# Softcap attention, ReLU² MLP and top-1 experts on one core: a division moved up, sixteen copies moved to ScalarE, the extra tile's weights in another order, and two small float32 products in float32r

## The chip, the core and the metric

The kernel runs on one core of a Trainium2 chip. TensorE multiplies (PE; its weight loads are a row of their own, PEld), VectorE (DVE) and ScalarE (ACT) do elementwise work, GpSimd (POOL) does a little of it and the indirect DMAs, and SyncE (SP) issues most of the other DMAs. The metric is the device time of the whole program in microseconds (us); lower is better. The time before is 510.29 us, the median of 3 runs (509.88 to 512.22). One more execution was taken with the profiler: it took 511.6 us, of which 509.9 us lie between its first and last instruction (the span, in which the trace counts its times).

## The reference

Three stages follow each other; the output of one is the input of the next. There are 2 x 448 = 896 tokens, 12 heads of 64, a model width of 768.

```python
# q, k, v: [2, 12, 448, 64]
scores = cap * tanh((q @ k.T) / 8 / cap)          # softcap attention, per head
attn = exp(scores - max); attn /= attn.sum(-1) + 1e-9
x = (attn @ v) as [896, 768]

h = maximum(x @ w_in, 0)                           # MLP: w_in [768, 2048], w_out [2048, 768]
x = (h * h) @ w_out

xn = x / (norm(x) + 1e-6); en = emb / (norm(emb) + 1e-6)   # 8 experts, top 1
logits = xn @ en.T / tau                           # [896, 8]
e = argmax(logits); gate = softmax(logits)[e]
out[row] = gate * (maximum(x[row] @ w1[e], 0) @ w2[e])     # w1 [8, 768, 1024], w2 [8, 1024, 768]
```

## The kernel before

**Number format.** A float32 matrix is held as two float32r tiles: a rounded high part (`xh`, `wh`, `gh`, ...) and the remainder (`xl`, `wl`, `gl`, ...). A product is three TensorE passes, high by high, high by low and low by high (`pass3`, lines 584 to 587). Small products whose operands are not split go to TensorE as plain float32.

**Stages.** The work is cut by batch b (0 and 1, 448 tokens each), and each stage of one batch is interleaved with the next stage of the other:

1. attention of batch 0 (12 heads, in 6 pairs, lines 376 to 574);
2. `mlp(0)` with attention of batch 1 between its matmuls;
3. `mlp(1)` with the router of batch 0;
4. `expert(0)` with the router of batch 1, and the preparation of the extra tile;
5. `expert(1)` with the extra tile.

`mlp(b)` has 16 h blocks (one per 128 columns of w_in: 6 x 3 matmuls of 448 columns, then ReLU and square) and 6 y blocks. `square` (line 598) squares on ACT, rounds the square into `gh` on DVE (line 603), and subtracts for `gl` on DVE (line 604). A block's square is issued when the next block has done three of its six steps.

**Attention.** A step g scores two blocks of keys (`scores`), prepares later heads (`fronts(g + 2)`: casts `qh`, `kh` and the transposed `tq`, mostly on DVE), and multiplies weights with v (`values(g)`, L471, plain float32). When a pair of heads m is complete, `divide(m)` (lines 483 to 493) reads the two PSUM banks of the pair on DVE: row sums `rs`, reciprocal, and two products into `rows`. Two steps later `finish(m)` (line 495) transposes `rows` on TensorE (`xp`, L508) into `xt`, the input of the MLP; its own remainder `xl` is written by DVE one step after (the `late` list). The banks that `divide` reads are the banks that the next pair's `values` write.

**Weights.** A chunk is a piece of a weight matrix. It passes the stages load (DMA on SP), conv (w_in and w_out lie in memory as 64-bit numbers and are turned into float32 by ACT L231 and DVE L214, L215, L217), store (of the float32 copy, for batch 1), and split (`wh` by ACT L237 or DVE L239, `wl` by DVE L243). `pump(n)` moves the stages of coming chunks on when chunk n is taken, and puts their instructions in a list; `drip` issues one of the list at each step of the main loop. Before `mlp(0)` the attention loop calls `pump` with n from -6 up to 0 (lines 1105 to 1108). From `expert(0)` on, even chunks lie in a pool of 2 buffers for each of `wf`, `wh` and `wl`, odd chunks in a pool of 4.

**Experts.** For each batch the expert that most of its tokens chose is computed densely for all 448 tokens: 20 chunks, 8 of w1 (`e` blocks, 18 matmuls each) and 12 of w2 (`z`, 6 column blocks of two chunks). So blocks 0 to 19 are batch 0, 20 to 39 batch 1. Tokens of other experts are gathered, 64 at a time, in an extra tile of its own weights: 12 chunks of w1 (128x512, products `xo`) and 8 of w2 (128x768, products `xy`). `XAT` (line 182) says after which block each of the 20 is used. `extra_next` (line 1167) lets the extra tile take one step at each block's end.

**The extra tile's rows** (`ys`, 64 rows) go to the output by an indirect DMA, except the last 256 columns of rows of batch 1: these are placed into the dense rows on TensorE by a 0/1 matrix `smt` (`extra_place`, line 961; `place`, line 1029, product `xm`, L1033, plain float32), and `merged_rows` adds the two.

**Router.** `router(b)` (line 744) multiplies x with the experts' vectors (`lg`, 12 float32r matmuls), and sums the squares of each token with a column of ones (L758, one plain float32 matmul of 448 columns into row 32 of the same bank). Two ACT copies and a POOL memset make `lgs`, which is transposed (`lt`).

What sets the order is the order of the Python code: instructions run in that order on each engine, and wait for each other by semaphores.

Of the kernel before, what the change touches and what calls it, by code (L numbers as in the profile page):

```python
# [20 lines left out]
def kernel(  # L21
# [34 lines left out]
    P = 128  # L56
# [125 lines left out]
    XAT = [18 + i for i in range(12)] + [31, 32, 32, 33, 33, 34, 34, 35]  # L182
# [193 lines left out]
    def attention():  # L376
# [175 lines left out]
        for g in range(G):  # L552
            if g + 2 < G:
                scores(g + 2)
                yield
                yield from fronts(g + 2)
                if g == 1:
                    guard()
            if g:
                yield from values(g)  # L560
            yield
            run_all(late)
            if todo:
                run_all(todo)
                yield
            if 2 <= g < G // 2:
                next(conv, None)
            if g == G // 2:
                run_all(late)
                yield "batch"  # L570
# [21 lines left out]
    def mlp(b):  # L592
# [5 lines left out]
        def square(f, r):  # L598
            if eng["sq"] == "act":
                nc.scalar.activation(r, r, AF.Square)  # L600
            else:
                nc.vector.tensor_tensor(r, r, r, op=ALU.mult)
            nc.vector.tensor_copy(gh[:, f], r)
            nc.vector.tensor_tensor(gl[:, f], r, f32(gh[:, f]), op=ALU.subtract)

        for f in range(NF):
            wh, wl = next_w()
            o = acc(f"h{b}_{f}")
            for cc in range(NCC):
                pass3(o[:, :S], wh[:, cc], wl[:, cc], xh[:, cc], xl[:, cc], cc == 0, cc == NCC - 1)  # L610
                if cc == 2 and late:
                    square(*late.pop())
                yield
            r = ev.tile([P, S], F32, tag="r", name=f"r{b}_{f}")
            nc.scalar.activation(r, o[:, :S], AF.Relu)  # L615
            late.append((f, r))
        square(*late.pop())
        x2h = xp.tile([P, NCC, S], F32R, tag="xh", name=f"x2h{b}")
# [61 lines left out]

    def router_setup():
# [12 lines left out]
        col = small([P, 1], "col")  # L694
        nc.gpsimd.memset(col, 1.0)
# [24 lines left out]
        e2 = small([P, NCC, 2, E], "e2", F32R)  # L720
        nc.vector.tensor_copy(e2[:, :, 0], tp)
        nc.vector.tensor_tensor(e2[:, :, 1], tp, f32(e2[:, :, 0]), op=ALU.subtract)
# [21 lines left out]
    def router(b):  # L744
# [5 lines left out]
        lg = bank("mm", f"lg{b}")  # L750
        for cc in range(NCC):
            w = e2[:, cc].rearrange("p t e -> p (t e)")
            nc.tensor.matmul(lg[:2 * E, :S], w, x2h[:, cc], start=cc == 0, stop=False)
            nc.tensor.matmul(lg[:2 * E, :S], w, x2l[:, cc], start=False, stop=cc == NCC - 1)
        yield

        NR = SQ + 1
        nc.tensor.matmul(lg[SQ:NR, :S], ent["col"], ssq[b], start=True, stop=True)  # L758
        lgs = ev.tile([NR, S], F32, tag="sq", name=f"lgs{b}", bufs=1)
        nc.gpsimd.memset(lgs[:SQ], 0.0)  # L760
        nc.scalar.copy(lgs[:2 * E], lg[:2 * E, :S])
        nc.scalar.copy(lgs[SQ:NR], lg[SQ:NR, :S])
# [5 lines left out]
        nc.vector.tensor_copy(ss, lt[:CP, :, SQ])  # L768
# [192 lines left out]
    def extra_place():  # L961
# [8 lines left out]
        yield  # L970
        tp = ps.tile([P, NC, CP], F32, tag="tr", name="smt_p", bufs=2)
        for c in range(NC):
            nc.tensor.transpose(tp[:T, c], sm[:, (B - 1) * NC + c], ident[:CP, :CP])
        yield
        smt = small([T, NC, CP], "smt")
        nc.vector.tensor_copy(smt, tp[:T])
# [19 lines left out]
    def expert(b, po):  # L996
# [32 lines left out]
        def place(d):  # L1029

            xm = ps.tile([P, NC, P], F32, tag="tr", name=f"xm{d}", bufs=2)
            for c in range(NC):
                nc.tensor.matmul(xm[:CP, c], rt["smt"][:, c], rt["done"][1][:, d * P:(d + 1) * P], start=True, stop=True)  # L1033
# [71 lines left out]
    for i, y in enumerate(att):  # L1105
        drip(2)
        if i >= PS and i % 6 == 0:
            pump(min((i - PS) // 6 - PB, 0))
# [125 lines left out]
```

## Time and profile before

| | |
|---|---|
| median of 3 runs | 510.29 us (509.88 to 512.22) |
| profiled execution | 511.6 us |
| its span | 509.9 us |
| PE busy | 498.4 us, 98% |
| PEld, DVE, ACT, POOL busy | 453.5, 384.8, 261.5, 72.1 us |
| DMA moved | 83.62 MB, mean 164 GB/s |
| chain that ended last | PE 86%, DVE 8%, DMA 3% |

How to read it: PE is busy from the first few microseconds to the last few. A busy PE can still be slowed, since a matmul's bar in the trace ends where the next has already started; what a matmul costs is read from one start to the next start. A stretch in which the starts lie farther apart than elsewhere is a loss that the busy share doesn't show.

### The profile page before, as it was taken

The page shows a single profiled execution, that of the slowest core. Times are in us where ns is not written, and L with a number is a line of the kernel's source. Part 1 is how long each engine was busy: PE and PEld are TensorE (multiplying, and loading weights), DVE is VectorE, ACT ScalarE, POOL GpSimd, SP SyncE. Part 2 cuts the span into 40 slices and gives each one's busy share as a digit, 9 for nine tenths or more (in the row PEclk, how much of TensorE's full clock was granted, in tenths as well). Part 3 has the DMA queues.
Part 4 walks back from the last instruction along what each step waited for, and adds up shares of the span by engine and source line. Part 5 has one row for each costly group of instructions (what it writes and reads, how often), then busy time and mean ns, then how long its engine had stood idle before and what let it go on. Part 6 is the DMA issues. An engine that isn't in the chain of part 4 may idle for free.

```text
span 509.9 us, 8176 instructions
## 1 busy us (share of the span) xinstructions
PE 498.4 (98%) x2814; PEld 453.5 (89%) x2814; DVE 384.8 (75%) x739; ACT 261.5 (51%) x420; POOL 72.1 (14%) x113
## 2 busy tenths in 40 slices
PE   8999999999999999999999999999999999999995
PEld 6899989899999999999998899999789899998984
DVE  6899999799998989896588477666557655456681
ACT  5989986887886674753143340011163213445341
POOL 3645432011110121002001000112100000000000
PEclk9999999999999999999999999999999999999998
DMA  8987959599576887885444123476523477645752
GB/s 127 195 192 161 226 131 244 175 271 279 179 187 200 239 233 207 241 247 160 140 119 125 44 83 95 87 171 179 138 61 74 111 165 166 192 147 158 202 153 55
DMA packets 166956, 83.62 MB, mean 164 GB/s; under 512 B 104050, under 2 KB 154098, under 8 KB 166912
## 3 DMA queue, kind: packets, MB, share of 16 engines
q1 hardware_dynamic: 165056, 82.68, 63.0%
q10 hardware_dynamic: 1728, 0.35, 0.3%
q8 instruction: 23, 0.38, 0.3%
q14 instruction: 21, 0.17, 0.2%
q0 software_dynamic: 128, 0.04, 0.0%
HBM read 65.12 MB, written 18.29 MB: 164 GB/s over the span
## 4 chain that ended last, share of the span: by engine, by line
PE 86%; DVE 8%; DMA 3%; issue 1%; ACT 1%; POOL 0%; DVEq 0%; SPq 0%; ACTq 0%; POOLq 0%
PE pv L471 8%; PE h L585 8%; PE y L585 8%; PE h L586 8%; PE h L587 8%; PE y L587 8%; PE y L586 8%; PE sc L447 5%; PE e L585 4%; PE e L587 4%; PE e L586 4%; PE z L585 3%; PE z L586 3%; PE z L587 3%; DMA wf<-in_moe_w_dram 2%
## 5 line engine op out<-in xcount | busy, mean ns | idle before, releaser
L243 DVE TENSOR_TENSOR wl<-wf,wh 128x512 fp32r<-128x512 f32 (+1 forms) x140 | 113.9, 827 | 43.3 <-ACT wh L237 40.0
L237 ACT CAST wh<-wf 128x512 fp32r<-128x512 f32 (+1 forms) x97 | 65.6, 697 | 39.9 <-PE z L587 25.4
L585 PE MATMUL h<-xh,wh 128*128 128x448 f32 x192 | 71.8, 374 | 0.0
L585 PE MATMUL y<-gh,wh 128*128 128x448 f32 x192 | 71.7, 374 | 0.0
L586 PE MATMUL h<-xh,wl 128*128 128x448 f32 x192 | 70.3, 366 | 0.0
L587 PE MATMUL h<-xl,wh 128*128 128x448 f32 x192 | 70.3, 366 | 0.0
L587 PE MATMUL y<-gl,wh 128*128 128x448 f32 x192 | 70.2, 366 | 0.0
L586 PE MATMUL y<-gh,wl 128*128 128x448 f32 x192 | 70.2, 366 | 0.0
L471 PEld LDWEIGHTS pv<-vt,p_t 128*112 128x112 f32 x576 | 63.1, 178 | 3.4 <-issue 1.4
L471 PE MATMUL pv<-vt,p_t 128*112 128x65 f32 x576 | 62.3, 259 | 1.0 <-issue 1.0
L449 ACT ACTIVATE p_t<-sc,rcap 128x448 f32<-128x448 f32 x84 | 49.2, 630 | 15.0 <-PE sc L447 15.0
L405 POOL TENSOR_TENSOR ql<-tq,qh 64x448 fp32r<-64x448 f32 x22 | 27.5, 1248 | 123.0 <-ACT qh L425 90.4
L453 ACT ACTIVATE p_t<-p_t,capb 128x896 f32<-128x896 f32 x41 | 42.8, 1045 | 1.3
L585 PEld LDWEIGHTS h<-xh,wh 128*128 128x128 f32 x192 | 36.1, 188 | 3.8 <-issue 0.8
L587 PEld LDWEIGHTS h<-xl,wh 128*128 128x128 f32 x192 | 36.1, 188 | 3.2
L587 PEld LDWEIGHTS y<-gl,wh 128*128 128x128 f32 x192 | 36.0, 188 | 3.1
L615 ACT ACTIVATE r<-h 128x448 f32<-128x448 f32 x32 | 17.3, 541 | 41.7 <-PE h L587 26.0
L586 PEld LDWEIGHTS h<-xh,wl 128*128 128x128 f32 x192 | 36.1, 188 | 2.9
L231 ACT ACTIVATE wf<-wr 128x512 f32<-128x512 f32 (+1 forms) x36 | 27.0, 750 | 22.6 <-DMA wr<-in_moe_w_out_dram 7.7
L586 PEld LDWEIGHTS y<-gh,wl 128*128 128x128 f32 x192 | 36.1, 188 | 2.7
L585 PEld LDWEIGHTS y<-gh,wh 128*128 128x128 f32 x192 | 36.1, 188 | 2.7
L447 PE MATMUL sc<-qh,kp 128*128 128x448 f32 x96 | 37.2, 388 | 1.0 <-DVE kp L419 0.4
(247 smaller groups left out, 911.0 us busy)
## 6 DMA issues: line engine op xcount, KB each, us to landing
wr<-in_moe_w_in_dram SPq DMA_DIRECT2D x16, 768.0 KB, 6.0
wr<-in_moe_w_out_dram SPq DMA_DIRECT2D x24, 512.0 KB, 4.7
wf<-in_moe_w_dram SPq DMA_DIRECT2D x24, 384.0 KB, 3.3
wf<-in_moe_w_dram SPq DMA_DIRECT2D x36, 256.0 KB, 3.4
wk<-wf SPq DMA_DIRECT2D x16, 384.0 KB, 6.1
wk<-wf SPq DMA_DIRECT2D x24, 256.0 KB, 4.5
wf<-wk SPq DMA_DIRECT2D x16, 384.0 KB, 4.1
wf<-wk SPq DMA_DIRECT2D x24, 256.0 KB, 3.2
```

The lines of the kernel that those rows point to most:

```text
L231: nc.scalar.mul(c["f"], c["parts"][:, :, :, 1].bitcast(F32), 2.0 ** -112)
L237: nc.scalar.copy(c["hi"], c["f"])
L243: nc.vector.tensor_tensor(c["lo"], c["f"], f32(c["hi"]), op=ALU.subtract)
L405: (nc.gpsimd if n > 1 else nc.vector).tensor_tensor(ql[D:], tq[:D], f32(qh[:D]), op=ALU.subtract)
L447: nc.tensor.matmul(sc[:, :S], h[0][:, c * P:(c + 1) * P], h[x], start=t == parts[0][0] and x == 1, stop=t == parts[-1][0] and x == 2)
L449: nc.scalar.activation(p_t[:, j], sc[:, :S], AF.Tanh, scale=rcap)
L453: nc.scalar.activation(p_t, p_t, AF.Exp, scale=capb)
L471: nc.tensor.matmul(o, w, x, start=i == 0 and t % 2 == 0, stop=i == NK - 1, skip_group_check=True)
L585: nc.tensor.matmul(o, wh, xh, start=first, stop=False)
L586: nc.tensor.matmul(o, wl, xh, start=False, stop=False)
L587: nc.tensor.matmul(o, wh, xl, start=False, stop=last)
L615: nc.scalar.activation(r, o[:, :S], AF.Relu)
```

## The change

Six edits; the tile shapes of the three stages and the number of their large matmuls stay.

1. In attention, at the last step of batch 0 (g + 1 = G/2) `fronts(g + 2)` is issued after `values(g)`, so after `divide`; in batch 1 `finish` is issued directly behind `values` and a step more lies between it and its `xl`.
2. The attention loop calls `pump` five times with n from -6 to -2; the two steps of n = -1 and 0 fall to the first `next_w` of `mlp(0)`.
3. In `mlp(0)` `gh` is written by ACT, and `gl` (new function `low`) is issued two steps later; `mlp(1)` is as before.
4. The router's sum of squares is split in a high and a low float32r part (`sh` by ACT, `sl` by DVE) and summed by two float32r matmuls into row 16 of the same product; one step more lies ahead of them. One ACT copy takes the place of two and of the memset.
5. `XAT` is another: the w1 chunks after blocks 18, 19, two each after 20 to 23, one each after 24 and 25; the w2 chunks one each after blocks 27 to 34 (before: w1 after 18 to 29, w2 after 31, 32, 32, 33, 33, 34, 34, 35).
6. The placement: `ys` (its last 256 columns) as high and low part in 128 rows `y2`, `smt` with 128 rows (each of the 64 twice), so that one float32r matmul takes the place of one float32 matmul. The transposes for it are issued one step earlier, and the copy of `smt` is by ACT.

```diff
-    XAT = [18 + i for i in range(12)] + [31, 32, 32, 33, 33, 34, 34, 35]
+    XAT = [18, 19, 20, 20, 21, 21, 22, 22, 23, 23, 24, 25] + [27 + i for i in range(8)]
...
                 scores(g + 2)
                 yield
-                yield from fronts(g + 2)
+                if g + 1 != G // 2:
+                    yield from fronts(g + 2)
...
             if g:
                 yield from values(g)
+            if g + 1 == G // 2:
+
+                yield from fronts(g + 2)
+            if g > G // 2 and todo:
+                run_all(todo)
+                yield
...
-            nc.vector.tensor_copy(gh[:, f], r)
+            if b:
+                nc.vector.tensor_copy(gh[:, f], r)
+                low(f, r)
+            else:
+                nc.scalar.copy(gh[:, f], r)
+                later.append((f, r))
+
+        def low(f, r):
             nc.vector.tensor_tensor(gl[:, f], r, f32(gh[:, f]), op=ALU.subtract)
...
                 if cc == 2 and late:
                     square(*late.pop())
+                if cc == 4 and later:
+                    low(*later.pop())
                 yield
...
+    NR = 2 * E + 1
...
-        col = small([P, 1], "col")
-        nc.gpsimd.memset(col, 1.0)
+        col = small([P, NR], "col", F32R)
+        nc.gpsimd.memset(f32(col), 0.0)
+        nc.gpsimd.memset(f32(col[:, NR - 1:]), 1.0)
...
         for cc in range(NCC):
-            w = e2[:, cc].rearrange("p t e -> p (t e)")
-            nc.tensor.matmul(lg[:2 * E, :S], w, x2h[:, cc], start=cc == 0, stop=False)
-            nc.tensor.matmul(lg[:2 * E, :S], w, x2l[:, cc], start=False, stop=cc == NCC - 1)
-        yield
-
-        NR = SQ + 1
-        nc.tensor.matmul(lg[SQ:NR, :S], ent["col"], ssq[b], start=True, stop=True)
-        lgs = ev.tile([NR, S], F32, tag="sq", name=f"lgs{b}", bufs=1)
-        nc.gpsimd.memset(lgs[:SQ], 0.0)
-        nc.scalar.copy(lgs[:2 * E], lg[:2 * E, :S])
-        nc.scalar.copy(lgs[SQ:NR], lg[SQ:NR, :S])
+            nc.tensor.matmul(lg, e2[:, cc], x2h[:, cc], start=cc == 0, stop=False)
+            nc.tensor.matmul(lg, e2[:, cc], x2l[:, cc], start=False, stop=False)
+        yield
+        sh = ev.tile([P, S], F32R, tag="sq", name=f"sh{b}", bufs=1)
+        sl = ev.tile([P, S], F32R, tag="xr", name=f"sl{b}")
+        nc.scalar.copy(sh, ssq[b])
+        nc.vector.tensor_tensor(sl, ssq[b], f32(sh), op=ALU.subtract)
+        yield
+        nc.tensor.matmul(lg, ent["col"], sh, start=False, stop=False)
+        nc.tensor.matmul(lg, ent["col"], sl, start=False, stop=True)
+        lgs = ev.tile([NR, S], F32, tag="xr", name=f"lgs{b}")
+        nc.scalar.copy(lgs, lg)
...
         rt["km"] = km
-        yield
+        y2 = small([2 * T, 2 * P], "y2", F32R)
+        yl = ys[:, DM - 2 * P:]
+        nc.scalar.copy(y2[:T], yl)
+        nc.vector.tensor_tensor(y2[T:], yl, f32(y2[:T]), op=ALU.subtract)
+        rt["y2"] = y2
+
+        s2 = small([CP, NC, 2, T], "s2")
+        nc.gpsimd.tensor_copy(s2, sm[:, g].unsqueeze(2).to_broadcast([CP, NC, 2, T]))
         tp = ps.tile([P, NC, CP], F32, tag="tr", name="smt_p", bufs=2)
         for c in range(NC):
-            nc.tensor.transpose(tp[:T, c], sm[:, (B - 1) * NC + c], ident[:CP, :CP])
-        yield
-        smt = small([T, NC, CP], "smt")
-        nc.vector.tensor_copy(smt, tp[:T])
+            nc.tensor.transpose(tp[:, c], s2[:, c].rearrange("p t k -> p (t k)"), ident[:CP, :CP])
+        yield
+        smt = small([2 * T, NC, CP], "smt", F32R)
+        nc.scalar.copy(smt, tp)
...
-                nc.tensor.matmul(xm[:CP, c], rt["smt"][:, c], rt["done"][1][:, d * P:(d + 1) * P], start=True, stop=True)
+                nc.tensor.matmul(xm[:CP, c], rt["smt"][:, c], rt["y2"][:, (d - NCC + 2) * P:(d - NCC + 3) * P],
+                                 start=True, stop=True)
...
-        if i >= PS and i % 6 == 0:
-            pump(min((i - PS) // 6 - PB, 0))
+        if i >= PS and i % 6 == 0 and i < PS + 6 * (PB - 1):
+            pump((i - PS) // 6 - PB)
```

What stands on the engines, at three places. The first is DVE at the end of batch 0's attention: `rs5` and `rows5` are `divide` of the last pair of batch 0, `qh14`, `tq15` and `kp15` prepare heads of batch 1. Before:

```order
L239 CAST wh1_894<-wf1001_447 128x768
L243 TENSOR_TENSOR wl1_896<-wf1001_447,wh1_894 128x768
L423 CAST qh14_839<-tq14_835 64x448
L386 STREAM_TRANSPOSE tq15_901<-qk14_728 128x448
L488 TENSOR_SCALAR rs5_917<-pv5_0_804,ecap_139 112x4
L488 TENSOR_SCALAR rs5_917<-pv5_1_805,ecap_139 112x4
L489 RECIPROCAL rs5_917<-rs5_917 112x8
L492 TENSOR_TENSOR rows5_916<-pv5_0_804,rs5_917 112x256
L492 TENSOR_TENSOR rows5_916<-pv5_1_805,rs5_917 112x256
L423 CAST kp15_903<-tq15_901 64x448
```

And now, on DVE at the same place:

```order
L239 CAST wh1_894<-wf1001_447 128x768
L243 TENSOR_TENSOR wl1_896<-wf1001_447,wh1_894 128x768
L488 TENSOR_SCALAR rs5_907<-pv5_0_804,ecap_139 112x4
L488 TENSOR_SCALAR rs5_907<-pv5_1_805,ecap_139 112x4
L489 RECIPROCAL rs5_907<-rs5_907 112x8
L492 TENSOR_TENSOR rows5_906<-pv5_0_804,rs5_907 112x256
L492 TENSOR_TENSOR rows5_906<-pv5_1_805,rs5_907 112x256
L423 CAST qh14_839<-tq14_835 64x448
L386 STREAM_TRANSPOSE tq15_916<-qk14_728 128x448
L423 CAST kp15_918<-tq15_916 64x448
```

The five instructions of the division stand ahead of the cast `qh14` and the transpose `tq15` instead of behind them. The second place is DVE some 25 us later, in `mlp(0)`: `rs6` and `rows6` are the division of batch 1's first pair, `wf7`, `wf8` and `wl5` weights, `gh0` and `gl0` the parts of a square. Before:

```order
L243 TENSOR_TENSOR wl5_1124<-wf5_965,wh5_1088 128x768
L217 SCALAR_TENSOR_TENSOR wf7_1077<-wr7_971,wf7_1077 128x768
L603 CAST gh0_962<-r0_2_1126 128x448
L604 TENSOR_TENSOR gl0_963<-r0_2_1126,gh0_962 128x448
L214 TENSOR_SCALAR wf8_1129<-wf8_1129 128x768
L488 TENSOR_SCALAR rs6_1170<-pv6_0_935,ecap_139 112x4
L488 TENSOR_SCALAR rs6_1170<-pv6_1_936,ecap_139 112x4
L489 RECIPROCAL rs6_1170<-rs6_1170 112x8
L492 TENSOR_TENSOR rows6_1169<-pv6_0_935,rs6_1170 112x256
```

And now:

```order
L243 TENSOR_TENSOR wl5_1124<-wf5_1014,wh5_1088 128x768
L217 SCALAR_TENSOR_TENSOR wf7_1077<-wr7_1021,wf7_1077 128x768
L214 TENSOR_SCALAR wf8_1129<-wf8_1129 128x768
L488 TENSOR_SCALAR rs6_1169<-pv6_0_935,ecap_139 112x4
L488 TENSOR_SCALAR rs6_1169<-pv6_1_936,ecap_139 112x4
L489 RECIPROCAL rs6_1169<-rs6_1169 112x8
L492 TENSOR_TENSOR rows6_1168<-pv6_0_935,rs6_1169 112x256
L492 TENSOR_TENSOR rows6_1168<-pv6_1_936,rs6_1169 112x256
L618 TENSOR_TENSOR gl0_957<-r0_2_1126,gh0_956 128x448
```

The cast `gh0` of block 2 has left DVE, and its `gl0` stands behind the division. The third place is ACT near the end, the casts `wh` of the chunks of batch 1's z blocks (128x512) and of the extra tile's w2 (128x768). Before:

```order
L237 CAST wh129_5005<-wf129_4927 128x768
L237 CAST wh130_5023<-wf130_4965 128x768
L237 CAST wh131_5032<-wf131_4981 128x512
L237 CAST wh132_5051<-wf132_4996 128x768
L237 CAST wh133_5062<-wf133_5009 128x768
L237 CAST wh134_5071<-wf134_5027 128x512
```

And now:

```order
L237 CAST wh129_4996<-wf129_4935 128x512
L237 CAST wh130_5005<-wf130_4950 128x768
L237 CAST wh131_5025<-wf131_4964 128x512
L237 CAST wh132_5034<-wf132_4979 128x768
L237 CAST wh133_5061<-wf133_5000 128x512
L237 CAST wh134_5070<-wf134_5015 128x768
```

Where two chunks of the extra tile stood for each z chunk there is now one.

## Rows read from the trace of the kernel before

**Rows 1.** The page, part 1: busy us, share of the span, instructions.

```profile
PE 498.4 (98%) x2814; PEld 453.5 (89%) x2814; DVE 384.8 (75%) x739; ACT 261.5 (51%) x420; POOL 72.1 (14%) x113
```

**Rows 2.** Waits of PE, whole span: the longest: us, times, longest.

```profile
PE xp L508 <- DVE rows L492: 1.3, 1, 1.3
```

**Rows 3.** Timeline, 66 to 72 us: start, us, engine, line, out<-in, [idle before].

```profile
68.18 0.38 DVE L423 CAST qh<-tq 64x448 fp32r<-64x448 f32 x1
...
68.64 1.13 POOL L405 TENSOR_TENSOR ql<-tq,qh 64x448 fp32r<-64x448 f32 x1 [3.38 <-DVE qh L423]
69.04 0.30 DVE L488 TENSOR_SCALAR rs<-pv,ecap 112x4 f32<-112x4 f32 x2
...
70.19 0.65 PE L508 MATMUL xp<-ident,rows 112*128 112x112 f32 x4 [1.27 <-DVE rows L492]
...
70.41 0.44 DVE L423 CAST kp<-tq 64x448 fp32r<-64x448 f32 x1
...
71.92 0.36 PE L447 MATMUL sc<-ql,kp 128*128 128x448 f32 x1
```

**Rows 4.** Timeline, 88 to 97 us, the division of pair 6.

```profile
89.71 0.92 ACT L231 ACTIVATE wf<-wr 128x768 f32<-128x768 f32 x1 [2.29 <-DVE wl L243]
...
93.98 0.39 DVE L603 CAST gh<-r 128x448 fp32r<-128x448 f32 x1 [3.44 <-ACT r L600]
...
95.16 0.37 PE L587 MATMUL h<-xl,wh 128*128 128x448 f32 x1
95.42 0.34 DVE L488 TENSOR_SCALAR rs<-pv,ecap 112x4 f32<-112x4 f32 x2
...
96.56 0.97 PE L471 MATMUL pv<-vt,p_t 128*112 128x65 f32 x8 [1.03 <-issue]
```

**Rows 5.** Timeline of PE, 280 to 282 us, the sum of squares of batch 0.

```profile
280.26 0.37 PE L587 MATMUL h<-xl,wh 128*128 128x448 f32 x1
280.56 0.91 PE L758 MATMUL lg<-sq,col 128*1 128x448 f32 x2
...
281.71 0.36 PE L586 MATMUL h<-xh,wl 128*128 128x448 f32 x1
```

**Rows 6.** Timeline of PE, 496 to 499 us, the first of two placements.

```profile
496.45 0.36 PE L587 MATMUL z<-hl,wh 128*128 128x448 f32 x1
496.74 1.12 PE L1033 MATMUL xm<-ys,smt 64*112 64x128 f32 x8
...
498.10 0.36 PE L586 MATMUL z<-hh,wl 128*128 128x448 f32 x1
```

**Rows 7.** The chain that ended last, 10 to 30 us: start, us, what.

```profile
17.21 1.53 PE pv L471 x16
```

**Rows 8.** Timeline, 482 to 488 us, extra tile's w2 beside the z blocks.

```profile
484.07 0.37 PE L587 MATMUL z<-hl,wh 128*128 128x448 f32 x1
...
485.15 0.34 PE L946 MATMUL xy<-wl,hh 128*128 128x384 f32 x1
485.33 0.33 PE L945 MATMUL xy<-wh,hh 128*128 128x384 f32 x1
...
486.57 0.83 ACT L237 CAST wh<-wf 128x768 fp32r<-128x768 f32 x1 [0.25 <-DMA wf<-in_moe_w_dram]
...
487.42 0.37 PE L587 MATMUL z<-hl,wh 128*128 128x448 f32 x1
```

**Rows 9.** Stretches: us, busy of PE, PEld, DVE, ACT, POOL, PEclk, DMA share, GB/s.

```profile
70.00:157.00 87.00, 85.78 (x505) 79.89 (x506) 80.89 (x129) 67.46 (x108) 13.89 (x19) 1.00 0.76 205
...
440.00:460.00 20.00, 20.00 (x98) 18.13 (x97) 10.02 (x16) 8.71 (x15) 0.00 (x0) 1.00 0.47 152
...
484.00:488.00 4.00, 3.64 (x16) 2.38 (x15) 2.77 (x4) 1.95 (x3) 0.00 (x0) 1.00 0.87 278
```

**Rows 10.** Copies of 128x448 by DVE and by ACT: ns min/median/max.

```profile
L603 DVE CAST gh<-r x32: 345/388/842, 80.0 to 305.7; 128x448 fp32r<-128x448 f32 x32
...
L509 ACT CAST xh<-xp x12: 517/534/537, 24.4 to 231.1; 128x448 fp32r<-128x448 f32 x12
```

More of the change, by code (lines that the diff above doesn't have):

```diff
@@ L602, in square @@
                 nc.vector.tensor_tensor(r, r, r, op=ALU.mult)
-            nc.vector.tensor_copy(gh[:, f], r)
+            if b:
[5 more added lines that the diff above has]
+        def low(f, r):
             nc.vector.tensor_tensor(gl[:, f], r, f32(gh[:, f]), op=ALU.subtract)
+        later = []
         for f in range(NF):
@@ L617, in mlp @@
         square(*late.pop())
+        if later:
+            low(*later.pop())
         x2h = xp.tile([P, NCC, S], F32R, tag="xh", name=f"x2h{b}")
@@ L719, in router_setup @@
         yield
-        e2 = small([P, NCC, 2, E], "e2", F32R)
-        nc.vector.tensor_copy(e2[:, :, 0], tp)
-        nc.vector.tensor_tensor(e2[:, :, 1], tp, f32(e2[:, :, 0]), op=ALU.subtract)
+        e2 = small([P, NCC, NR], "e2", F32R)
+        nc.gpsimd.memset(f32(e2[:, :, 2 * E:]), 0.0)
+        nc.vector.tensor_copy(e2[:, :, :E], tp)
+        nc.vector.tensor_tensor(e2[:, :, E:2 * E], tp, f32(e2[:, :, :E]), op=ALU.subtract)
         ent["e"] = e2
@@ L749, in router @@
         e2 = ent["e"]
-        lg = bank("mm", f"lg{b}")
+        lg = bank("mm", f"lg{b}")[:NR, :S]
         for cc in range(NCC):
-            w = e2[:, cc].rearrange("p t e -> p (t e)")
-            nc.tensor.matmul(lg[:2 * E, :S], w, x2h[:, cc], start=cc == 0, stop=False)
-            nc.tensor.matmul(lg[:2 * E, :S], w, x2l[:, cc], start=False, stop=cc == NCC - 1)
+            nc.tensor.matmul(lg, e2[:, cc], x2h[:, cc], start=cc == 0, stop=False)
+            nc.tensor.matmul(lg, e2[:, cc], x2l[:, cc], start=False, stop=False)
         yield
-        NR = SQ + 1
-        nc.tensor.matmul(lg[SQ:NR, :S], ent["col"], ssq[b], start=True, stop=True)
-        lgs = ev.tile([NR, S], F32, tag="sq", name=f"lgs{b}", bufs=1)
-        nc.gpsimd.memset(lgs[:SQ], 0.0)
-        nc.scalar.copy(lgs[:2 * E], lg[:2 * E, :S])
-        nc.scalar.copy(lgs[SQ:NR], lg[SQ:NR, :S])
+        sh = ev.tile([P, S], F32R, tag="sq", name=f"sh{b}", bufs=1)
[7 more added lines that the diff above has]
+        nc.scalar.copy(lgs, lg)
         yield
@@ L767, in router @@
         ss = small([CP, NC], f"ss{b}")
-        nc.vector.tensor_copy(ss, lt[:CP, :, SQ])
+        nc.vector.tensor_copy(ss, lt[:CP, :, NR - 1])
         yield
```

## The prediction

> **What bounds the kernel now.** I read the busy line first: PE 98%, every other engine at most 75% [rows 1]. So only what shortens PE's own row counts, or what keeps it from lengthening. Of the waits of PE the longest is 1.27 us, of `xp` for the division's product [rows 2, 3]; its waits alone would leave little to gain. But a bar of PE ends where the next begins, so next I read start-to-start distances. Where nothing disturbs it a main matmul takes 0.2 us (98 of them in the 20 us from 440 to 460, 0.204 [rows 9]); I use 0.205. Against that the timelines show five places where the distance is longer: the end of attention of batch 0 [rows 3], the first division of batch 1 [rows 4], the two sums of squares [rows 5], the two placements [rows 6], and the blocks in which the extra tile takes two chunks of w2 [rows 8]. The change touches all five, and nothing else on PE's row. All of the following is counted against the profiled execution: 511.6 us, of which 509.9 are span; it lies 1.3 above the median of 510.29.
>
> **Division moved up (edit 1).** On DVE `qh14` starts at 68.18 and the division at 69.04 [rows 3]; once the division stands first it starts 0.86 earlier, and `xp` with it: of its wait of 1.27 some 0.41 stays, the rest goes. What is late next: `qh14` now stands behind the division, which holds DVE from 69.04 to 70.41, 1.37 in all. POOL's `ql` takes 1.13 and had waited for `qh` (idle 3.38 before it); it moves from 68.64 to 70.01 and ends at 71.14. PE wants it for the `sc` that stood at 71.92, now at 71.06: a new wait of about 0.1. I take -0.7; the ends are -1.3 (the `xp` wait gone whole) and 0 (POOL's span is rough, and `kp15` behind the transpose may be what is late).
>
> **The division that stood behind a square (edit 3).** At 90.54 DVE comes to `gh` of block 2 and stands 3.44 us, since ACT has not squared that block yet; the division behind it starts at 95.42, and PE, which began its last matmul at 95.16, starts `pv` at 96.56 [rows 4]: 1.40 instead of 0.20, so 1.20 lost. After the change `gh` is ACT's and `gl` stands behind the division. The next thing the division waits for is the weight piece `wf8`: ACT writes it from 89.71 to 90.63. From `gh` to the division DVE needed 1.44 (93.98 to 95.42), which I take whole although the two instructions on the square, the longer part of it, leave; the division then starts by 92.1 (90.63 + 1.44), and PE may go on 1.14 behind that (95.42 to 96.56), at 93.2. PE wants it at 95.36, less the 0.7 gained before, 94.65. 1.4 us of slack, so -1.2; ends 0 and -1.2. The extra work is ACT's: 16 copies at 0.534 instead of 0.388 on DVE [rows 10], 8.5 us. ACT is busy 67.46 of the 87 us of this stretch [rows 9]; it goes to about 76 (87%), DVE from 80.89 to 74.7. I price it at nothing, because PE is the busy engine there (85.78 of 87); the last rival says what it costs if that cover is gone.
>
> The Trainium skill speaks against that move: by "VectorE: DVE Perf Modes", section "The perf-mode tier table (the rule you actually need)", a float32 copy inside SBUF is one of the few operations that VectorE does at double rate, while a subtraction of two tensors is not, so the move takes VectorE's cheap instruction and leaves it the dear one. The rows agree (0.388 against 0.534); it matters only if ACT is the one that is late.
>
> **Sum of squares (edit 4), twice.** From the L587 at 280.26 to the second L586 behind it at 281.71 there are 1.45 us [rows 5]; two ordinary matmuls (the L587, and one L585 that isn't shown) hold 0.41 of it, so the float32 product costs 1.04. Two float32r matmuls of 448 columns cost 2 x 0.205 = 0.41. Gain 0.63 each, -1.26 for both batches; ends 0 (each float32r matmul as dear as half of the float32 one, 0.52) and -1.26. `sh`, `sl` are made a step ahead of use, by engines with idle time in rows 9.
>
> **Placement (edit 6), twice.** In the same way 496.45 to 498.10 is 1.65, less 0.41: 1.24 for eight float32 pieces of 128 columns [rows 6]. Now four matmuls. Nearest row for a short matmul with 112 weight columns: 16 pieces of `pv` in 1.53, 0.096 each [rows 7]. So 4 x 0.096 = 0.39, a gain of 0.85 each, -1.7. The other end: a piece at 1.24/8 = 0.155 and a float32r matmul as dear as two, a gain of 0. I take -1.7, since `pv` has fewer moving columns (65) and as many weights, and still 0.096: what counts is not the moving part.
>
> On that the Trainium skill, "TensorE: Matmul & The Clock Gate", section "Back-to-back issue gap", gives about 81 ns for sustained matmuls of 128 columns; by it four cost 0.32 and the two gains would be 1.84 together. The `pv` row's 96 ns with half the moving columns disagrees, and its section "LDWEIGHTS (loading the stationary operand)", weight columns over 1.2, says 93 ns for 112: with the row. I keep the row.
>
> **One w2 chunk of the extra tile per block (edit 5).** From 484.07 to 487.42 [rows 8] are 3.35 us. In it lie three main matmuls (0.62) and eight of `xy` at 0.18 less overlap, 0.176 (1.41; two of them are shown 0.18 apart): 2.0 us of work, 1.34 lost. There ACT's cast waits for a DMA (idle 0.25 before 486.57), DMA engines are 87% busy and 278 GB/s flow [rows 9]. Such a block needs two extra chunks (128x768, 393 KB each) and a dense one (128x512, 262 KB), 1048 KB, while PE has the 1.41 of `xy` and 12 matmuls of z, 2.46, to do: 271 GB/s wanted, beside what the kernel stores. With one extra chunk per block it is 655 KB in 2.46 + 0.70 (half of 1.41) = 3.16 us: 207 GB/s. I take the whole -1.34; ends 0 and -1.34. The price is paid at w1: there two extra chunks (128x512, 262 KB each) come with one dense chunk (393 KB) in an e block of 18 x 0.205 = 3.7 us without `xo`: 917 KB, at most 248 GB/s, where 152 flow now [rows 9]. That is under the 278 that the trace shows as possible, so I price it at nothing.
>
> **Small things (edits 2 and 6).** Two steps of weight loading fall to `mlp(0)`, near 70 us; the piece they touch is `wf8`, which has the 1.4 of slack above. Near the end a subtraction and the wider transposes are new; at most one copy of 0.53 [rows 10] that is late, taken 0.2.
>
> **Sum.** -0.7 -1.2 -1.26 -1.7 -1.34 +0.2 = -6.0: span 503.9, profiled time 505.6, median 510.29 - 6.0 = 504.3 us.
>
> **Rivals.**
> - *Half of the gains don't come.* The wait at 95 us takes another releaser (ACT's casts come 0.53 later behind each new copy, so `wf8` is late too), and the placement goes at the fp32 price. For it: the slack of 1.4 rests on a DMA that landed just then. Against: of ACT's idle 19.5 us a part lies right there (2.29 before 89.71). Then 504.3 + 1.2 + 0.85 = 506.3. Chance 0.23.
> - *The pairs of w1 are late instead of the pairs of w2.* Five blocks with two extra chunks; if each loses about what the w2 pair lost beyond its rate, half of 1.34 = 0.7, that is 3.5 and 507.8: no change. For it: casts and landings queue the same way on ACT and DVE. Against: 152 GB/s and DVE 10 of 20 us busy in that stretch [rows 9]. Chance 0.10.
> - *ACT becomes the bound in the h blocks of batch 0: slower.* ReLU, square, `gh`, softcap and weight casts are one queue on ACT; per h block 76/16 = 4.75 us of work. If its present idle time of 19.5/16 = 1.2 stays in full (it waits for DVE, DMA and PE in turn, and no gap can take the copy), a block takes 6.0 us where PE has 85.8/16 = 5.35. That is +0.65 x 16 = 10.5, less the gains outside this stretch (1.26 + 1.7 + 1.34): 510.3 + 10.5 - 4.3 = 516.5. It decides from the point at which a ReLU comes later than PE's need of that PSUM bank. Against: 87% leaves 11 us of room. Chance 0.05.
>
> **How the numbers follow.** My forecast has 0.62, the rivals 0.23, 0.10, 0.05. A measurement of this kernel tells no less than 0.5% (2.55 us) from no change, so faster means under 507.7, slower over 512.8. The forecast and the first rival are faster, 0.85, less 0.01 for the first rival's tail; that 0.01 and the second rival are no change, 0.11; the last is slower, 0.05. Range: at the low end all terms at their better ends (-1.3 -1.2 -1.26 -1.7 -1.34 = -6.8, so 503.5) and twice the 0.41 by which the fastest run of before lies under its median: 502.7. The high end lies just past the second rival, 508.0; outside are the last rival and half of the second.
>
> **What the new profile would show.** Right: no PE wait for `rows` near 69 over 0.5 us, and a short one of `sc` for `ql` behind it; no `pv` wait near 95; the two `lg` matmuls with `col` 0.205 apart; four `xm` about 0.1 apart; z blocks from 478 on without ACT waiting for a DMA; ACT at 87% in batch 0's h blocks, PE still without gaps there; span near 503.9. Wrong: a PE wait for a ReLU's bank or for `gl` (L618) in that stretch; `xo` matmuls that wait for L237 or L243 between blocks 20 and 23; `ql` on POOL ending past 71.3.

## The result and the profile after

The changed kernel takes 504.94 us (median of 4 runs, 504.79 to 506.79) where the kernel before takes 510.12 (median of 4 runs; 510.29 was that of the first three). The ratio on record is 0.9889, with a 95% interval of 0.9863 to 0.9916; the two medians alone give 0.9898. By the medians that is 5.2 us less; the forecast was 6.0 less, 504.3 us, within 502.7 to 508.0. The profiled execution took 504.95 us, its span is 503.2.

The page, part 1, and three rows of PE's waits (total us, times, longest):

```profile
PE 494.6 (98%) x2806; PEld 453.5 (90%) x2806; DVE 379.3 (75%) x724; ACT 271.5 (54%) x439; POOL 74.0 (15%) x114
```

```profile
PE idle L146 <- DVE zero L143: 1.5, 1, 1.5
PE ot L1077 <- ACT of L1107: 0.4, 1, 0.4
PE sc L447 <- POOL ql L405: 0.3, 1, 0.3
```

PE is as busy in share as before, over a span that is 6.7 us shorter. The waits of `xp` [rows 2] and of `pv` [rows 4] are gone. What is left stands in the first 16 us or at the end; the 0.3 for `ql` is no new wait (it stands at 14.6 us, in the kernel before at 14.3). The 1.5 at the very start, ahead of the first matmuls (`idle`, on zeros), is in the kernel before too, where it was longer than the wait of `xp`. The end of batch 0's attention, in the order of time, as [rows 3] of before:

```profile
67.92 0.35 DVE L488 TENSOR_SCALAR rs<-pv,ecap 112x4 f32<-112x4 f32 x2
...
69.11 0.65 PE L508 MATMUL xp<-ident,rows 112*128 112x112 f32 x4
69.21 0.38 DVE L423 CAST qh<-tq 64x448 fp32r<-64x448 f32 x1
...
69.67 1.15 POOL L405 TENSOR_TENSOR ql<-tq,qh 64x448 fp32r<-64x448 f32 x1 [4.67 <-DVE qh L423]
...
70.62 0.37 PE L447 MATMUL sc<-qh,kp 128*128 128x448 f32 x1
...
70.87 0.47 PE L447 MATMUL sc<-ql,kp 128*128 128x448 f32 x1
```

`xp` starts without a wait; `ql` ends at 70.8, and its `sc` starts 0.25 after the one before it instead of 0.2 (the next start behind it comes 0.1 late as well, so 0.15 in all). Then the division of batch 1's first pair, as [rows 4]:

```profile
87.86 0.91 ACT L231 ACTIVATE wf<-wr 128x768 f32<-128x768 f32 x1
...
91.51 0.34 DVE L488 TENSOR_SCALAR rs<-pv,ecap 112x4 f32<-112x4 f32 x2
91.89 0.20 DVE L489 RECIPROCAL rs<-rs 112x8 f32<-112x8 f32 x1
92.13 0.76 DVE L492 TENSOR_TENSOR rows<-pv,rs 112x256 f32<-112x256 f32 x2
92.80 0.62 DVE L618 TENSOR_TENSOR gl<-r,gh 128x448 fp32r<-128x448 f32 x1
```

```profile
94.14 0.37 PE L594 MATMUL h<-xl,wh 128*128 128x448 f32 x1
94.35 0.91 PE L471 MATMUL pv<-vt,p_t 128*112 128x65 f32 x8
```

The division ends at 92.9, `pv` starts at 94.35, right behind the matmul ahead of it. The sum of squares and the first placement on PE, as [rows 5] and [rows 6]:

```profile
280.89 0.36 PE L594 MATMUL h<-xl,wh 128*128 128x448 f32 x1
281.09 0.37 PE L784 MATMUL lg<-sh,col 128*17 128x448 f32 x1
281.30 0.37 PE L785 MATMUL lg<-sl,col 128*17 128x448 f32 x1
281.50 0.36 PE L592 MATMUL h<-xh,wh 128*128 128x448 f32 x1
281.70 0.37 PE L593 MATMUL h<-xh,wl 128*128 128x448 f32 x1
```

```profile
491.47 0.37 PE L594 MATMUL z<-hl,wh 128*128 128x448 f32 x1
491.68 0.52 PE L1065 MATMUL xm<-y,smt 128*112 128x128 f32 x4
492.03 0.42 PE L592 MATMUL z<-hh,wh 128*128 128x448 f32 x1
492.29 0.37 PE L593 MATMUL z<-hh,wl 128*128 128x448 f32 x1
```

From the last main matmul ahead to the second behind are 0.81 us where 1.45 were (sum), and 0.82 where 1.65 were (placement). The first stretch of [rows 9], the one with the four pairs of w1 chunks (blocks 20 to 23, products `xo` from 428.5 to 443.1 us), and one of z blocks with one chunk of w2 each:

```profile
70.00:157.00 87.00, 87.00 (x512) 81.11 (x512) 76.66 (x116) 78.12 (x127) 16.57 (x21) 1.00 0.78 217
424.00:444.00 20.00, 20.00 (x97) 17.81 (x95) 11.49 (x18) 9.94 (x17) 0.00 (x0) 1.00 0.73 202
466.00:482.00 16.00, 16.00 (x82) 14.98 (x81) 9.50 (x14) 6.14 (x9) 0.00 (x0) 1.00 0.80 211
```

PE has no gap in any of them; ACT is busy 78.1 of 87 us in batch 0's h blocks, 90% (forecast 87%).

### The profile page after: what moved, and what is told of

Same layout as the page of the kernel before. It is cut to its first block, busy times and chain, and to the rows that moved or that the text cites. A ratio compares the mean times of both kernels' runs of the same rounds, so it can differ in the third digit from the quotient of the medians.

```text
span 503.2 us, 8180 instructions
## 1 busy us (share of the span) xinstructions
PE 494.6 (98%) x2806; PEld 453.5 (90%) x2806; DVE 379.3 (75%) x724; ACT 271.5 (54%) x439; POOL 74.0 (15%) x114
## 4 chain that ended last, share of the span: by engine, by line
PE 96%; DVE 1%; DMA 1%; ACT 0%; POOL 0%; issue 0%; DVEq 0%; ACTq 0%; POOLq 0%
PE pv L471 13%; PE h L592 8%; PE y L592 8%; PE y L594 8%; PE h L594 8%; PE h L593 8%; PE y L593 8%; PE sc L447 7%; PE e L592 4%; PE z L592 4%; PE e L593 4%; PE e L594 4%; PE z L593 4%; PE z L594 4%; PE xp L508 1%; DMA qk<-in_q_dram 1%
## 5 line engine op out<-in xcount | busy, mean ns | idle before, releaser
L243 DVE TENSOR_TENSOR wl<-wf,wh 128x512 fp32r<-128x512 f32 (+1 forms) x140 | 112.6, 815 | 36.7 <-ACT wh L237 32.8
L652 POOL TENSOR_TENSOR sq<-sq,sq 128x448 f32<-128x448 f32 x10 | 13.3, 1330 | 159.8 <-ACT sq L650 159.8
```

The source lines that it names most:

```text
L243: nc.vector.tensor_tensor(c["lo"], c["f"], f32(c["hi"]), op=ALU.subtract)
L652: nc.gpsimd.tensor_tensor(ssq[b], ssq[b], sq, op=ALU.add)
```

## The experiments

All times are medians; each ratio is to runs of the kernel before on the same chip, with its 95% interval, as recorded (the two medians alone can give up to 0.14% more or less). A "wait" of PE is the distance between two starts less the usual one for that matmul.

**The kernel before, profiled again.** No edit.

> The kernel before once more, unchanged, to get a second profile of it. Its first profile took 511.6 us, 1.5 above the median of its runs, and the wait of 1.3 us in the block with two w2 chunks of the extra tile was read from that profile alone. Theory A (the wait belongs to the order of the chunks): the new profile has 1.2 to 1.4 us of it again, whatever its total time, and the 1.5 lie elsewhere. Theory B (the wait was an accident of the one profiled execution): a profile at 509.9 to 510.3 us has under 0.3 us of it, and the edit of the chunks is worth nothing in the median. Time in both: 510.1, ratio 1.000.

Measured 510.26 us, ratio 0.9996 (0.9982 to 1.0009); the profiled execution took 509.77. Its w2 block, from 483.36 to 485.49, lost 0.1 us, not 1.3 ([rows 8] has 3.35 us for the same matmuls), and the wait of `pv` near 95 us was 0.83, not 1.20:

```profile
89.13 0.92 ACT L231 ACTIVATE wf<-wr 128x768 f32<-128x768 f32 x1 [1.91 <-DMA wr<-in_moe_w_in_dram]
...
94.97 0.37 PE L587 MATMUL h<-xl,wh 128*128 128x448 f32 x1
96.00 0.97 PE L471 MATMUL pv<-vt,p_t 128*112 128x65 f32 x8 [0.67 <-issue]
```

```profile
483.36 0.37 PE L587 MATMUL z<-hl,wh 128*128 128x448 f32 x1
...
485.49 0.36 PE L587 MATMUL z<-hl,wh 128*128 128x448 f32 x1
```

Theory B is right in that the w2 wait comes and goes from one execution to the next (1.3, 0.1, 0.8, 0.4, 0.2, 0.7, 0.2 and 0.6 us in the eight profiles of this record with the old order, mean 0.5); that the edit would then be worth nothing is the next run's matter. The wait at 95 us varies too (1.20, 0.83, 0.46, 0.62, 0.35 in five profiles that have that stretch unchanged). That of `xp` is 1.0 to 1.4 in the six profiles without edit 1, mean 1.3, and 0.0 to 0.45 in the eight with it, mean 0.2.

**Edit 5 alone.**

```diff
-    XAT = [18 + i for i in range(12)] + [31, 32, 32, 33, 33, 34, 34, 35]
+    XAT = [18, 19, 20, 20, 21, 21, 22, 22, 23, 23, 24, 25] + [27 + i for i in range(8)]
```

> The kernel before with edit 5 alone (the order of the extra tile's chunks). Theory A: 510.1 - 1.3 = 508.8 us, ratio 0.9974, and no DMA wait in the z blocks. Theory B: 510.1, ratio 1.000. Rival C (the pairs of w1 are late instead): 510.1 - 1.3 + 3.5 = 512.3, with waits of PE in the blocks 20 to 23 of batch 1.

Measured 509.5 us, ratio 0.9987 (0.9976 to 0.9998), which is -0.7 us: between A and B, as a wait of 0.1 to 1.3 would give. No block from 20 to 23 shows a wait for a weight, so rival C falls.

**Edits 4 and 6 alone** (the hunks on `lg`, `lgs`, `y2`, `smt` of the diff above, nothing else).

> The kernel before with edits 4 and 6 alone (sums of squares and placement in float32r). In the trace of the changed kernel the two sums cost 0.64 less each and the two placements 0.83 less each: if these four places are all, 510.1 - 2.9 = 507.2 us, ratio 0.9942. Rival: the float32 pieces left other work time that is missing afterwards (a copy or a weight that comes later than PE), and part of it returns: 508 to 510.

Measured 509.03 us, ratio 0.9970 (0.9958 to 0.9982): -1.5, half of the 2.9. The rival is right. On PE the four places cost what they cost in the changed kernel. What is lost lies behind PE's last matmuls: from the last four transposes `ot` to the end of the span are 7.95 us here, and 6.05 in both profiles of the kernel before and in that of the changed kernel. The tail experiments below take this up.

**Edits 1 to 3 alone.**

> The kernel before with edits 1, 2 and 3 alone (the division moved up, the steps of weight loading, gh by ACT). The trace of the changed kernel shows the wait of xp gone whole (1.4), 0.15 new behind ql, and the 1.2 near 95 us gone: 510.1 - 2.5 = 507.6 us, ratio 0.9951. Rival: of the wait of xp only the 0.7 of the forecast goes in the median of the runs, since PE's start differs from run to run against DVE's: 508.3.

Measured 508.66 us, ratio 0.9970 (0.9958 to 0.9981): -1.5 (ratio) to -1.8 (medians), nearer to the rival than to the -2.5 of the theory, which had priced both waits by one profile. In its trace 0.16 is left of the wait of `xp` and nothing of that of `pv`.

**Edit 1 alone** (the two hunks in the attention loop: `fronts` behind `values`, `finish` directly behind `values`).

> The kernel before with edit 1 alone (division of the last pair ahead of the next heads). Profiles with this edit show the wait of xp at 0 to 0.3 instead of 0.9 to 1.3, and 0.15 new behind ql. Theory: 510.3 - 1.0 = 509.3 us, the wait of pv near 95 unchanged at 0.3 to 1.2. Rival (the forecast's 0.7, or a later wait takes it back): 509.6 to 510.3.

Measured 513.22 us, ratio 1.0070 (1.0047 to 1.0093): slower by 2.9 (medians) to 3.6 us (ratio), which neither theory had. The wait of `xp` is down to 0.28, and that of `pv` has grown to 3.1:

```profile
90.65 0.92 ACT L231 ACTIVATE wf<-wr 128x768 f32<-128x768 f32 x1 [4.21 <-DMA wr<-in_moe_w_in_dram]
```

```profile
93.77 0.37 PE L592 MATMUL h<-xh,wh 128*128 128x448 f32 x1
94.32 0.57 ACT L607 ACTIVATE r<-r 128x448 f32<-128x448 f32 x1
94.92 0.40 DVE L610 CAST gh<-r 128x448 fp32r<-128x448 f32 x1 [3.19 <-ACT r L607]
...
96.36 0.34 DVE L488 TENSOR_SCALAR rs<-pv,ecap 112x4 f32<-112x4 f32 x2
...
97.51 1.71 PE L471 MATMUL pv<-vt,p_t 128*112 128x65 f32 x8 [2.96 <-issue]
```

Read from below: `pv` waits for the division, the division stands behind `gh`, `gh` waits for the square on ACT, and the square stands behind the conversion of a weight that waits for its DMA. From that conversion to `pv` it is always the same time: 89.71 to 96.56 in [rows 4], 89.13 to 96.00 in the second profile of before, 90.65 to 97.51 here: 6.85, 6.87, 6.86 us. In three more profiles without edits 1 to 3 it is 6.84 to 6.86. The row of [rows 4] names `wl` on DVE as what ended ACT's idle time, but the traces put the landing of that load 0.07 to 0.08 ahead of the conversion in all three (89.63, 89.06 and 90.57), while in the second profile the `wl` in question ends only behind it. So `pv` was tied to the landing of a weight, not to PE. Here the landing came later by about 1.2 us (the conversion by 0.94 and 1.52 against the two profiles of before): the load takes as long (6.8 us, before 7.2 and 6.9), but is issued at 83.74 instead of 82.43 and 82.15, and so is the load ahead of it (77.13 instead of 75.74 and 75.55). PE came earlier by 0.9 (its last matmul starts at 94.18 against 95.16 and 94.97). Both lengthen the wait. And it costs once more (stretches, columns as in [rows 9]: the granted clock is the third number from the end):

```profile
94.00:96.00 2.00, 0.54 (x3) 0.16 (x1) 1.04 (x3) 2.00 (x4) 0.00 (x0) 1.00 0.83 218
96.00:98.00 2.00, 0.49 (x3) 0.52 (x4) 1.93 (x7) 1.31 (x3) 0.00 (x0) 0.88 0.86 325
98.00:100.00 2.00, 2.00 (x10) 1.91 (x10) 2.00 (x3) 0.00 (x0) 0.00 (x0) 0.50 0.06 24
```

Behind the 3 us in which PE stood still the clock goes to 0.50, 1.2 GHz: the matmuls that follow start 0.37 apart instead of 0.2. The 8 pieces of `pv` take 1.46 to the next start instead of 0.72, and the five matmuls behind them 0.9 more in all: 1.6 us. With the wait at 3.1 instead of 0.7 and 1.1 less of `xp` that makes +2.9. That it falls after idle time is what the Trainium skill says in "TensorE: Matmul & The Clock Gate", section "What's actually happening"; the trace agrees here, and a second fall, at the start of the run below with edit 5 undone and no scatter, follows a wait of 1.0 us. How wait and clock share the loss is shown for the profiled execution alone: five of the six executions have a mean granted clock of 0.991 to 0.994, but one has 0.997 and took about as long as the profiled one (512.84 and 512.92 us).

**Edit 3 alone** (`gh` of batch 0 by ACT, `gl` two steps later).

> The kernel before with edit 3 alone (gh of batch 0 by ACT, gl two steps later). The wait near 95 us was 1.20 in the first profile of before, and 0.83, 0.46, 0.62 and 0.35 in four other profiles of kernels that have that stretch unchanged: mean 0.7. Theory: 510.3 - 0.7 = 509.6 us, no wait of pv near 95, the wait of xp near 70 unchanged at 1.1 to 1.3. Rival (the forecast's 1.2 as read from the first profile): 509.1.

Measured 509.86 us, ratio 0.9995 (0.9981 to 1.0010). The wait of `pv` is gone in its trace, that of `xp` is 1.0. The interval holds both no change and the theory's -0.7; more than that it can't tell. Edits 1 and 3 alone make +2.9 and about -0.4, together with edit 2 -1.5 to -1.8: edit 1 pays only with the others. Which of edits 2 and 3 it needs was not tried. Edit 2 moves the weight loads too: in the changed kernel the load on which the division hung is issued at 81.15 and lands at 87.78, 1.85 us earlier than in the first profile of before. An estimate from the rows above: with that conversion at 87.86 and the 6.86 us from it to `pv`, the wait without edit 3 would be about 0.4 (94.72 against 94.35).

**gh back on DVE, but late.** In the changed kernel:

```diff
-                nc.scalar.copy(gh[:, f], r)
                 later.append((f, r))
...
         def low(f, r):
+            if not b:
+                nc.vector.tensor_copy(gh[:, f], r)
```

> The changed kernel with gh of batch 0 on DVE again, but issued together with gl, two steps behind the square. Theory P (the place in DVE's queue counts, not the engine): DVE no longer stands at gh ahead of the division, so the wait near 95 us stays away: 504.9 us within 0.5, ACT back to about 69 of the 87 us. Rival (ACT's copy is what helps, since DVE with 16 x 0.39 more is late elsewhere): a wait of PE for gl or for a division in batch 0's h blocks, 505.5 to 507 us.

Measured 504.94 us, ratio 0.9904 (0.9883 to 0.9924), no change against the changed kernel (that the medians agree to the last digit is chance). `pv` has no wait near 95 us. ACT falls to 69.8 of 87 us, DVE rises to 82.5:

```profile
70.00:157.00 87.00, 87.00 (x514) 81.14 (x513) 82.52 (x133) 69.83 (x112) 16.77 (x21) 1.00 0.81 224
```

So the place in DVE's queue is what counts, not the engine: theory P. (`xp` waited 0.45 in this profile, which took 505.59; that is at 69.6 us, ahead of the first `gh`.)

**Each gh copied twice by ACT**, in the changed kernel.

```diff
                 nc.scalar.copy(gh[:, f], r)
+                nc.scalar.copy(gh[:, f], r)
```

> The changed kernel with each of the 16 copies gh on ACT done twice (the same output), to price the forecast's slower rival: 16 x 0.55 = 8.8 us more on ACT, which was 78.1 of 87 us busy there, so 87 of 87. Rival D (ACT's present gaps can't take work; it bounds at once): +8.8 less nothing, 512 to 514 us. Theory of the forecast (the gaps take most of it, ACT's queue is late only at single places): +1 to +4, 506 to 509 us, with new waits of PE for p_t or for weights, not for every ReLU.

Measured 506.58 us, ratio 0.9939 (0.9917 to 0.9961): +1.6 for 16 more copies of 0.57. There is one new wait of PE, for a ReLU at 144.5 us:

```profile
PE h L592 <- ACT r L634: 1.2, 1, 1.2
```

So ACT's gaps take 16 copies at no cost that these runs show, and 32 for 1.6 us; the forecast's slower rival (10.5 us, a gap that takes no work) is far off.

**The changed kernel with edit 5 undone.** The line XAT as in the kernel before.

> The changed kernel with edit 5 undone (old order of the extra tile's chunks). In the trace of edits 4 and 6 alone the last stores of orow stood behind the landing of the scatter of ys, which waits for the stores of oq; the end came 7.9 us after the last transposes of PE, against 6.1 in before and in the changed kernel. Theory T (the tail): edit 5 is worth more here than in before, since it brings the scatter forward as well; undone it costs the w2 wait (0.1 to 1.3 in four profiles, mean 0.6) and 1.0 to 1.9 of tail: 504.9 + 2.0 = 506.9 us, scatter landing less than 1 us before the last orow is ready. Rival (the edits add up, edit 5 is worth what it was worth alone, 0.7): 505.6 us.

Measured 507.17 us, ratio 0.9943 (0.9925 to 0.9961): edit 5 is worth 2.2 us here, three times what it is worth alone, near theory T. And PE is not the place (its w2 block lost 0.2). The last transposes start at the same time as in the changed kernel; the chains of the two kernels have

```profile
497.17 0.45 PE ot L1077 x2
```

with the old order and

```profile
497.20 0.44 PE ot L1077 x2
```

in the changed kernel, but the spans are 505.3 and 503.2. Old order, POOL's scatter, SP's last stores, and the time from issue to landing of these stores:

```profile
495.82 0.97 POOL L982 DMA_INDIRECT out_dram<-ys,ixu  x1 [93.72 <-DVE orow L1079]
```

```profile
498.29 1.34 SPq L1082 DMA_DIRECT2D out_dram<-orow  x3
```

```profile
DMA to landing us min/median/max: 2.3/2.6/3.7
```

and in the changed kernel:

```profile
494.92 0.97 POOL L982 DMA_INDIRECT out_dram<-ys,ixu  x1 [92.97 <-DVE orow L1079]
```

```profile
497.39 1.86 SPq L1082 DMA_DIRECT2D out_dram<-orow  x3
```

```profile
DMA to landing us min/median/max: 2.0/2.1/2.2
```

The scatter takes 2.3 us to land in both, and the first store of `orow` goes 0.14 behind that. With the old order it is 0.9 later, and all four last stores (three by SP, one by ACT) go within 1.4 us. The last of them goes 0.3 later than in the changed kernel and takes 3.7 us to land instead of 2.0: 2.1 us at the end.

Why the scatter is later, the traces show too. In all twelve profiles that have it, it starts 1.08 to 1.09 us behind the landing of the last store of `oq`. With the old order that store goes 0.9 later, because DVE comes to the transpose ahead of it 0.9 later; just ahead of it DVE still prepares the extra tile's rows (from 488.0 us). Old order, then the changed kernel:

```profile
490.07 0.64 DVE L1056 STREAM_TRANSPOSE ot<-z 128x448 f32<-128x448 f32 x1
```

```profile
489.18 0.64 DVE L1056 STREAM_TRANSPOSE ot<-z 128x448 f32<-128x448 f32 x1
```

**Edits 5 and 6 alone.**

> The kernel before with edit 5 and edit 6 alone (order of the chunks, placement in float32r). Edit 5 alone gave -0.7, edits 4 and 6 together -1.5, of which the two sums of squares should be 1.3. Theory T: with the scatter brought forward the placement pays its 1.66 in full: 510.3 - 0.7 - 1.66 = 508.0 us, end 6.1 us after the last transposes. Rival (the placement is worth only what is left, 0.2 to 0.3, whatever the order): 510.3 - 0.7 - 0.3 = 509.3 us.

Measured 508.36 us, ratio 0.9959 (0.9940 to 0.9977): -2.1 (by the medians -1.7), nearer to the theory's 2.3 than to the rival's 1.0; the end comes 6.1 us behind the last transposes, as theory T has it.

**Edit 5 undone, without the scatter.** `extra_scatter` issues nothing, so the extra tile's rows are missing in the output.

> The changed kernel with the old order of the extra tile's chunks, and without the indirect DMA that scatters the extra tile's rows to the output (those rows are missing in the output). With the scatter this kernel took 507.2 us; its last transposes on PE start at 497.17, as in the changed kernel (497.20), and all its loss lies behind them. Theory T (the stores of orow stand behind the scatter's landing): without the scatter the loss goes, 505.0 us, span 503.1, end 6.0 us behind the last transposes. Rival (the stores themselves take longer, since several are in flight at once, whoever released them): 506.5 to 507.2.

Measured 505.79 us, ratio 0.9914 (0.9896 to 0.9932), 1.4 less than with the scatter; its end comes 6.0 us behind the last transposes again (498.59 to 504.6), as in theory T. The time lies between the theory's 505.0 and the rival's 506.5. What is missing to 505.0 is on PE in this profile, whose execution took 506.29: its w2 block lost 0.6, and PE fell 1.2 behind the run with the scatter in its first 25 us, where it waited 1.0 for `qh` and the granted clock stood at 0.50 from 7.8 to 14.6 us (the clock is the third number from the end):

```profile
PE sc L447 <- ACT qh L414: 1.0, 1, 1.0
```

```profile
8.00:10.00 2.00, 2.00 (x8) 1.80 (x8) 1.89 (x5) 1.78 (x4) 0.00 (x0) 0.50 0.59 91
```

What the other five executions lost (505.34 to 506.71) no trace shows.

**The changed kernel without the scatter.** The same rows missing.

> The changed kernel without the scatter alone (the same rows are missing). In its trace the scatter lands at 497.25, the first store of orow goes at 497.39, and SP then waits 0.64 us for the last piece of orow. Theory T: the scatter is just out of the way here, 504.9 us, within 0.3. Rival (the scatter still holds the end back): 504.0 or less.

Measured 505.04 us, ratio 0.9902 (0.9884 to 0.9921): no change, so in the changed kernel the scatter is out of the way, by the 0.64 that SP waits for the last piece of `orow`. And it is the scatter that holds these stores: without it the first goes at 494.66 instead of 497.39.

```profile
494.66 4.77 SPq L1079 DMA_DIRECT2D out_dram<-orow  x3
```

## Why the prediction was right, and where its terms were not

The direction, the size and the five places were right; the two profiles show on PE -1.3 (division), -1.2 (`pv`), -1.27 (two sums), -1.66 (two placements), -1.3 (w2 block) and +0.39 at the start, where PE's first `sc` came later: -6.3 of the span's -6.7. But the medians differ by 5.2, and some terms reached the end by another way than I gave. That the total came so near is in part luck: two terms were read from waits that were near their longest, one was too small, and edit 5 made up for them at a place that the forecast did not look at.

- **Division moved up, -0.7: too small, and wrong alone.** I let 0.41 of the wait of `xp` stay; in this profile DVE was 0.26 earlier and PE 0.33 later at that point, so nothing stayed (0.2 in the mean of the eight profiles with edit 1), and 0.15 is new at `ql` (forecast 0.1). By the means of the profiles the term is -1.0. What the forecast missed is that the gains hang together: I counted the division and the wait at 95 us as two gains that don't know of each other. In the changed kernel they do add. But the second wait hung on a weight's landing, so that PE's being earlier only lengthened it, and edit 1 alone is 3 us slower. The forecast's own sentence had it (need at 95.36 "less the 0.7 gained before"), but only for the slack, not for what edit 1 would be without edits 2 and 3.
- **The division behind a square, -1.2: mechanism right, size from an unlucky execution.** The division starts at 91.5 (forecast: by 92.1) and there is slack of 1.4 us, as forecast. But five profiles give the wait as 0.35 to 1.20, mean 0.69. That the copy went to ACT was not needed (the run with `gh` back on DVE); that `gh` leaves the place ahead of the division is enough (edit 3 alone has no such wait).
- **Sums, -1.26: right.** 0.64 and 0.63 measured on PE.
- **Placement, -1.7: right on PE, not foreseen at the end.** 0.83 and 0.84 less. By the forecast's own measure the four matmuls cost 0.82 less 0.41, 0.41 (forecast 0.39). From the first start to the next main matmul's they take 0.35, 0.088 each (forecast 0.096; the Trainium skill's 81 ns of "TensorE: Matmul & The Clock Gate", section "Back-to-back issue gap", and the `pv` row lie on either side); that main matmul then takes 0.05 longer. The step that is missing is the way from PE to the end: I took every microsecond of PE for one of the span. The last stores stand behind the scatter's landing, which hangs on the stores of `oq` and not on PE's last matmuls. With the old order of chunks 1.4 to 2.1 of the gain are lost there.
- **One w2 chunk per block, -1.34: about the right size for the wrong reason.** The wait that I read was as long as that in one of eight profiles; alone the edit is worth 0.7. In the changed kernel it is worth 2.2, nearly all of it because the scatter comes 0.9 earlier. The price at w1 was nothing, as forecast: 202 GB/s from 424 to 444, where the pairs lie (forecast: at most 248), and no wait.
- **Small things, +0.2:** nothing of it is seen where the forecast put it. But the forecast had no term for the start. PE's first `sc` starts at 6.24 to 6.66 us in the seven profiles with edit 4 and at 5.92 to 6.18 in the seven without, 0.4 later in the mean. The load of q that DVE's first transpose waits for is issued at the same time in the two kernels' profiles, but the transpose starts at 4.90 us instead of 4.35. Why is not shown.

The sum with the mean waits and the later start (-1.0 -0.7 -1.27 -1.66 -0.5 +0.4) is -4.7, an estimate from the profiles, beside the measured 5.2 (the interval is 4.3 to 7.0). The profile that I summed from had both of its chance waits at their longest, 1.3 us above their means together, which by this estimate is why its execution took 511.6 us.

## What to carry to other kernels

A wait read in one profile is a sample: where a DMA's landing releases it, profile the same kernel twice before pricing the edit that removes it, and follow the wait back to what fixes its time, because an edit that only brings the waiting engine earlier then gains nothing or loses. Time taken from the bound engine counts only if the other chain to the end (here scatter, then stores behind it in one queue) has slack; look for it in the last microseconds first.

## What the runs showed of the hardware that was not expected

- PE's pace for the same stream of main matmuls has two values, and it changes in mid-stream. In the kernel before, h blocks of batch 1 (18 matmuls) take 3.65 us up to block 5 and 3.72 in blocks 12 to 15; in the changed kernel both take 3.65, while its main matmuls from 380 to 390 us start 205.9 ns apart, where those of before start 202.5 apart. In that stretch the seven profiles with edit 4 have 204.6 to 205.9 and the seven without 202.5 to 202.7, although edit 4's sum of squares lies 12 us ahead of it; what selects the pace was not tried. Over the span both kernels lose about the same by it: 1.7 (before) and 1.6 us (changed) against 202.6 ns per matmul, and 1.3 to 2.1 in the experiments.
- The wait of 3 us in the run of edit 1 alone cost 1.6 us more than itself, by the clock at 0.50 behind it. The waits of `xp` of 1.0 to 1.4 us show no such fall, but a wait of 1.0 us at the start of the run with edit 5 undone and no scatter does, so the length of a single wait does not tell.
- The four last stores of `orow` took up to 3.7 us to land when they were issued within 1.4 us, and 2.0 to 2.2 when they were spread over 1.9 us (the changed kernel with the old and with the new order).
